# Attention output of three batches: transposed by DMA through a DRAM scratch instead of on TensorE

## The chip, the cores and the metric

One Trainium2 chip, one of its cores. The metric is the device time of one execution in microseconds (us). The kernel before took 310.94 us, the median of three runs (310.38 to 312.49).

## What is computed

Eight batches of masked attention, eight heads each, feed a two-layer network with SiLU between the layers:

```
B, H, S, D = 8, 8, 576, 64
scores = scale * q @ k.T                      # per batch and head, 576 x 576
mask_plain: 0 <= rel < 32                     # heads 0..3
mask_dil:   0 <= rel < 128 and rel % 4 == 0   # heads 4..7
attn = softmax(where(mask, scores, -1e9));  o = attn @ v
x = o.transpose(0, 2, 1, 3).reshape(4608, 512)
h = x @ w_in;  g = h * sigmoid(h);  out = g @ w_out      # 512 -> 2048 -> 512
```

Here rel is the row position minus the column position. Only a narrow band of the scores is nonzero, so the attention is cut into small blocks.

## The kernel before

**Tiles.** Everything but the accumulators is in fp16. The weights, the q and k of two batches and a ring xA stay on chip. xA holds x transposed, 128 partitions x 4 column blocks x 2048 tokens, that is the last four token groups of 512. The first layer reads it as the moving operand: `h_g_f` is one of 16 slices of the first layer of group g, four matmuls at line 895. There are ten groups: two of 256 tokens, eight of 512.

**Attention of a batch.** The score blocks (`s`, line 638) go through exp on ScalarE (lines 647 and 651) and a mask product on VectorE (line 657). The products with v are `av_p` (six plain ones of 96 rows, `P` steps) and `av_d` (two halves of four residues of 72 rows, `D` steps). All are issued at line 684. VectorE divides each by its sum (lines 687 and 688) and writes the result to `oP`, 96 x 6 x 4 x 64, or `oD`, 72 x 2 x 4 x 4 x 64. There is one oP and one oD for all batches.

**From o to x.** `oP` and `oD` hold tokens on partitions; the first layer needs features there. `x_p` (steps `XP`, line 712) transposes the 96 rows of one plain block with two TensorE transposes into PSUM. `x_d` (steps `XD`, line 728) transposes half of the dilated heads with eight. ScalarE or VectorE then copies the PSUM tile into xA (lines 516 and 518), whichever the planner thinks is free first. Per batch that makes 12 plain and 16 dilated transposes.

**q and k.** For batches 0 to 2 they are transposed on TensorE. From batch 3 on, POOL casts them to fp16 into a DRAM scratch `kq_s` (line 156), and SP issues four DMA transposes per batch from it: two into `nat` (plain heads, line 170) and two into `kqT` (dilated heads, line 173). This is a "turn". When a turn has landed, a small copy on POOL into `fence` (line 459) lets the loads of the next batch go (v, then the casts of q and k).

**Order.** The order of every engine's instructions is fixed when the kernel is built. A planner (`Plan`) keeps a modelled clock and picks the next TensorE step among attention steps, first-layer steps and second-layer steps, when its inputs and its PSUM bank are modelled as ready. DMA steps are entered with a modelled time (`yield "DMA", us`), and a first-layer step of a group depends on the steps listed in `spans` for its tokens. Each engine then executes its own list in order, and waits on semaphores for the real events. SP's list holds one load at the start and the turns of batches 3 to 7.

**Layer two.** The first two groups use plain products (line 930). The others use a scheme with seven products of halves (`y0`, `y1`, line 1005, eight matmuls per step), whose sums of operands are made on VectorE (line 966), and whose results leave through ScalarE copies (lines 1025 and 1035), VectorE additions (line 1032) and stores on ScalarE's queue (line 1037).

Of the kernel before, what the change touches and what calls it, by code (L numbers as in the profile page):

```python
# [9 lines left out]
F16 = mybir.dt.float16  # L10
# [6 lines left out]
def kernel(  # L17
# [9 lines left out]
    nc = tc.nc  # L27
    B, H, S, D = q.shape
    DM, DFF = moe_w_in.shape
    P = 128  # L30
    W = 32
    DIL = 4
    M = S // DIL
    MH = M // 2
# [3 lines left out]
    QB = P - W  # L38
    NB = S // QB
    HP = H // 2  # L40
    HN = H // 2
# [6 lines left out]
    VA, VB = 80, M - 112  # L48
    scale = 1.0 / (D ** 0.5)
    PEB = 3  # L50
    GA = 4
    NA = GA * GT
    HT = GT // 2
# [14 lines left out]
    dram = ctx.enter_context(tc.tile_pool(name="dram", bufs=1, space=bass.MemoryType.DRAM))  # L68
# [11 lines left out]
    w_out16 = cpool.tile([P, NFF, DM], F16, name="w_out16")  # L80
    xA = cpool.tile([P, HP, GA * GT], F16, name="xA")
    NP = 8
# [6 lines left out]
    oP = cpool.tile([QB, NB, HN, D], F16, name="oP")  # L89
    oD = cpool.tile([MH, 2, DIL, HN, D], F16, name="oD")  # L90
# [28 lines left out]
    mask_p = cpool.tile([P, 6, QB], F16, name="mask_p")  # L119
    mask_d = cpool.tile([P, 10, MH], F16, name="mask_d")  # L120

    kq_s = {b: dram.tile([2, H * S * D], F16, name=f"kq_s{b}") for b in range(PEB, B)}

    def nat_of(b, key):
# [4 lines left out]
    def kq_plain(b):  # L129
        t = nats[b % 2]  # L130
        return t[:, : LEAD + NW], t[:, LEAD + NW : LEAD + 2 * NW]

    def issue_nat(b, h0, h1):
        for nm, src, m0 in (("k", k, 0), ("q", q, MR)):
            rows = src[b].rearrange("h (m r) d -> m h (r d)", r=DIL)
            r0 = M - MR if nm == "k" else 0
            p0 = 0 if nm == "k" else MR
            for d, at in ((nat_of(b, nm), m0), (nat_of(b, "rest")[p0 : p0 + MR], r0)):
                nc.gpsimd.dma_start(
                    out=d[:, h0:h1].rearrange("p h r d -> p h (r d)"),  # L140
                    in_=rows[at : at + d.shape[0], h0:h1],
                )
# [18 lines left out]
    def issue_turn(b, n):  # L161
        i = n % 2
        flat = kq_s[b][i]
        if n < 2:
            if b < PEB + 2 and i == 0:
                nc.gpsimd.memset(kq_plain(b)[0][:, :LEAD], 0.0)
# [69 lines left out]
    for t in probs:  # L236
        c = 2 * 4 * MH
        n = PW + P - c
# [6 lines left out]
    for what in ORDER:  # L245
        kind, n = what[0], int(what[1])
# [4 lines left out]
        elif kind == "o":  # L251
            nc.gpsimd.dma_start(
                out=w_out16[:, 4 * n : 4 * n + 4], in_=wo[:, 4 * n : 4 * n + 4]
# [22 lines left out]
    def third_batch():  # L276
        for n in range(2, PEB):
            issue_nat(n, 0, H)
        issue_vraw(2)
        issue_vp(2)  # L280
        issue_cast(PEB)
        yield "DMA", 0.0
# [109 lines left out]
    plan = Plan()  # L392
# [15 lines left out]
    def count(key, n, then):  # L408
        counts[key] = counts.get(key, 0) + 1
        if counts[key] == n:  # L410
            then()
# [22 lines left out]
    need = {g: (t0 + n - 1) // S for g, (t0, n) in enumerate(GROUPS)}  # L434
    v_in = {b: Step(None, 0.0) for b in range(3, B)}
    turned = {b: Step(None, 0.0) for b in range(PEB, B)}

    def x_of(g):
        t0, n = GROUPS[g]
        return xA[:, :, t0 % NA : t0 % NA + n]  # L440

    def turn_gen(b):
        for n, us in enumerate((3.0, 3.0, 1.5, 7.5)):
            issue_turn(b, n)
            yield "DMA", us
        for n in (b, b + 1) if b == 3 == PEB else (b + 1,):
            if n < B:
                count(("L", n), loads_need(n), lambda n=n: start_loads(n))

    def loads_need(b):  # L450
        return 1 + (b > PEB or b == 3)
# [22 lines left out]
    def start_loads(b):  # L474
        plan.push(Step(None, 0.0), loads_gen(b), plan.now)

    def attention(b):
# [10 lines left out]
            kqT = kqTs[b % 2]  # L488
        probs_of = {}
        steps = {}  # L490
        def small(ring, shape, dt, name):
            return POOLS[ring].tile(shape, dt, tag=ring, name=name)

# [198 lines left out]
        def av_p(ring, j):  # L692
            def lhs(i):
                return prob_cols(("p", j, i // 2), i % 2)

            yield from av(
                ring, f"p{j}", oP[:, j], rcps[:, j], lhs, lambda i: vp[:, i * NB + j, : D + 1]
            )

        def av_d(ring, ab, r):  # L700
            def lhs(i):
                return prob_cols(("d", ab, r // 2, i), r % 2)

            yield from av(
                ring, f"d{ab}{r}", oD[:, ab, r], rcps[:, NB + ab * DIL + r], lhs,
                lambda i: vd[:, ab, i, r, : D + 1],
            )

        def x_p(ring, j):
            xp = small(ring, [P, HP // 2, QB], F16, f"xp_{b}_{j}")  # L710
# [29 lines left out]
        if b == 0:  # L740
            order = [
# [7 lines left out]
            ]  # L749
        elif b < ORD:  # L750
            order = [
# [6 lines left out]
            ]  # L758
        elif pe_path:
            order = [  # L760
# [7 lines left out]
            ]  # L768
        else:
            order = [  # L770
# [4 lines left out]
            ]  # L775
        for key in order:
            kind, a = key[0], key[1:]
            rings = ["x", "z"] + (["h", "y", "u"] if b == 0 else ["h"] if b < 2 else [])
# [7 lines left out]
            elif kind == "TA" and b == 0:  # L786
                st = Step(
                    lambda ring, a=a: trans_a0(ring, *a), 0.36, rings,
# [8 lines left out]
            elif kind == "TA":  # L797
                st = Step(
                    lambda ring, a=a: trans_a(ring, *a), 0.36, rings,
                    [steps["N", "k"], steps["N", "rest"]], ("ACT",),  # L800
                )
            elif kind == "TB":
                st = Step(
                    lambda ring, a=a: trans_b(ring, *a), 0.18, rings, [steps["N", "q"]], ("ACT",)
# [3 lines left out]
            elif kind == "S":  # L808
# [10 lines left out]
                else:  # L819
                    deps = [steps["TD", h] for h in range(HN)]  # L820
                st = Step(
                    lambda ring, a=a: scores(ring, *a), 0.17 + 0.32 * (b in BIASED), ["s", "hh"] + (["xz"] if pe_path else []),
# [4 lines left out]
            elif kind == "P":  # L827
                us = sorted({home["p", a[0], hp][0] for hp in range(HP // 2)})
                st = Step(
                    lambda ring, a=a: av_p(ring, *a), 0.13, rings,  # L830
# [3 lines left out]
            elif kind == "D":  # L834
                us = sorted({home["d", a[0], a[1] // 2, h][0] for h in range(HN)})
                st = Step(
                    lambda ring, a=a: av_d(ring, *a), 0.13, rings,
# [4 lines left out]
            else:  # L842
                st = Step(
                    lambda ring, a=a: x_d(ring, *a), 0.28, rings,
# [30 lines left out]
        spans = [  # L875
            (b * S + QB * key[1], b * S + QB * (key[1] + 1), steps[key])
            for key in order if key[0] == "XP"
        ] + [
            (b * S + DIL * MH * key[1], b * S + DIL * MH * (key[1] + 1), steps[key])
            for key in order if key[0] == "XD"  # L880
        ]
        return [steps[key] for key in order], spans

    gTs = {}
# [178 lines left out]
    spans = []  # L1063
# [12 lines left out]
    for c in WPARTS:  # L1076
        w_steps["sums", c] = Step(
            lambda ring, c=c: w_sums(c), 0.0, (), [max(AT_WOUT)], ("DVE",)
        )
        w_steps["last", c] = Step(  # L1080
            lambda ring, c=c: w_last(c), 0.0, (), [st for _, st in l2] + [w_steps["sums", c]], ("DVE",)
        )
    sums += [w_steps[key, c] for key in ("sums", "last") for c in WPARTS]
    n = 0
# [38 lines left out]
    while att or l1 or l2:  # L1123
# [27 lines left out]
        for q_, it, lim in cands:  # L1151
            r = plan.ready(it[1])
# [4 lines left out]
            if it[1].mate:  # L1157
# [3 lines left out]
                r = max(r, r2)  # L1161
            r = max(r, plan.t + plan.backlog(it[1].uses) - lim)
# [45 lines left out]
```

## Time and profile before

| | |
|---|---|
| median of the runs | 310.94 us |
| the profiled execution | 311.68 us |
| its span, first to last instruction | 309.9 us |
| TensorE / weight loads busy | 297.2 / 198.5 us |
| VectorE / ScalarE busy | 196.0 / 190.9 us |
| h matmuls, line 895 | 142.4 us in 640 |
| plain transposes, line 712 | 96 matmuls, 206 ns median each |
| dilated transposes, line 728 | 128 matmuls, 197 ns median each |
| copies into xA from xp / xd | 50 (32 ScalarE, 18 VectorE) / 36 (27, 9) |
| DMA transposes nat / kqT, issue to landing | 7.0 / 5.1 us median |

The page gives the busy time of each engine in one profiled execution, and a chain of waits followed back from the last instruction. The length of a matmul in the trace runs from its first read to its modelled end, and successive matmuls overlap; so what a group takes of TensorE's time is read from its start to the start of the next group. In timelines, a bracket at the end of a line gives the idle time before it and what ended it. `SPq`, `ACTq` and `POOLq` are the queues that issue DMAs.

The attention of batches 5, 6 and 7 stands at about 145 to 172, 174 to 202 and 205 to 232 us of the span; the h and y steps of groups 4 to 7 are interleaved with it.

### The profile page before, as it was taken

Reading aid. Unit: us, or ns where it says so; the run is one execution under the profiler, and the core shown is the slowest. Engines: PE = TensorE matmul, PEld = TensorE weight load, DVE = VectorE, ACT = ScalarE, POOL = GpSimd, SP = SyncE. Lnnn points to the kernel's source line nnn. Section 1 sums busy time; section 2 is a strip of 40 time slices with the busy share of each in tenths; the row PEclk is TensorE's granted clock in tenths of the full one; section 3 lists DMA queues with packets and bytes.
Section 4 is the critical chain, followed back from the end, with each engine's and each line's share of the span. In section 5 each row is a group of like instructions: output and inputs, shape, how many; then the busy total and the mean of one; then the engine's idle time right before and its main releaser. Section 6 shows DMA issues by size and latency. Waiting matters only on the chain.

```text
span 309.9 us, 7152 instructions
## 1 busy us (share of the span) xinstructions
PE 297.2 (96%) x2910; PEld 198.5 (64%) x2910; DVE 196.0 (63%) x550; ACT 190.9 (62%) x400; POOL 55.4 (18%) x83
## 2 busy tenths in 40 slices
PE   7899999989999999999999999999999999999995
PEld 3468765654567666756765775576558656756884
DVE  6278999889958784787668757666684044105411
ACT  7567783488687649668666785586572455355320
POOL 8845732001640150050005000000000000000000
PEclk9999999999999999999999999999999999999999
DMA  8999999999999999989999991101001101100131
GB/s 105 183 201 196 203 189 204 213 201 143 127 142 185 206 114 225 223 107 183 247 146 93 193 238 31 36 36 68 2 0 70 69 2 68 70 0 35 42 130 68
DMA packets 89344, 38.69 MB, mean 125 GB/s; under 512 B 61280, under 2 KB 84704, under 8 KB 89312
## 3 DMA queue, kind: packets, MB, share of 16 engines
q0 software_dynamic: 48528, 19.86, 52.6%
q1 hardware_dynamic: 35600, 8.95, 19.1%
q10 hardware_dynamic: 5184, 9.44, 8.8%
q8 instruction: 22, 0.36, 0.5%
q14 instruction: 10, 0.08, 0.1%
HBM read 39.81 MB, written 15.34 MB: 178 GB/s over the span
## 4 chain that ended last, share of the span: by engine, by line
PE 80%; DVE 10%; ACT 4%; DMA 2%; issue 1%; ACTq 1%; POOL 1%; POOLq 0%
PE h L895 35%; PE y L1005 28%; PE y L930 4%; PE s L638 3%; PE av_d L684 2%; DMA nat<-in_q_dram 2%; PE av_p L684 2%; DVE gT L909 2%; PE xp L712 2%; DVE probs L657 1%; PE s L626 1%; PE xd L728 1%; DVE work L966 1%; DVE ob L1032 1%; ACT probs L647 1%
## 5 line engine op out<-in xcount | busy, mean ns | idle before, releaser
L895 PE MATMUL h<-xA,w_in 128*128 128x512 f16 (+1 forms) x640 | 142.4, 357 | 1.8 <-ACT probs L651 0.9
L904 ACT ACTIVATE gT<-h 128x512 f16<-128x512 f32 x116 | 68.7, 597 | 43.8 <-PE h L895 42.6
L895 PEld LDWEIGHTS <-w_in 128*128 128x128 f16 x640 | 56.8, 97 | 41.2 <-issue 2.5
L1005 PEld LDWEIGHTS <-gT 128*128 128x128 f16 x512 | 49.2, 98 | 9.4 <-issue 0.4
L1032 DVE TENSOR_TENSOR ob<-y,nat 128x256 f32<-128x256 f32 x48 | 20.3, 422 | 52.2 <-PE y L1005 48.5
L1005 PE MATMUL y<-w_out,gT 128*128 128x256 f16 x384 | 48.0, 273 | 0.1
L1005 PEld LDWEIGHTS <-work 128*128 128x128 f16 x384 | 36.7, 98 | 8.9 <-issue 2.0
L1005 PE MATMUL y<-w_sum,work 128*128 128x256 f16 x256 | 31.9, 272 | 0.8 <-ACT ob L1035 0.5
L684 PEld LDWEIGHTS <-probs 128*128 128x128 f16 x448 | 23.2, 99 | 12.8 <-DVE oP L688 1.9
L647 ACT ACTIVATE probs<-s 128x768 f16<-128x768 f32 (+2 forms) x31 | 24.5, 789 | 8.3 <-PE s L638 4.4
L688 DVE TENSOR_TENSOR oD<-av_d,rcps 72x256 f16<-72x256 f32 x64 | 26.9, 421 | 2.2
L1025 ACT COPY nat<-y 128x256 f32<-128x256 f32 x48 | 17.8, 380 | 12.7 <-PE y L1005 12.5
L907 ACT ACTIVATE th<-h 128x256 f32<-128x256 f32 (+1 forms) x44 | 19.2, 445 | 7.2 <-PE h L895 4.7
L909 DVE SCALAR_TENSOR_TENSOR gT<-th,h 128x256 f16<-128x256 f32 (+1 forms) x44 | 20.6, 487 | 2.2 <-ACT th L907 2.1
L688 DVE TENSOR_TENSOR oP<-av_p,rcps 96x256 f16<-96x256 f32 x48 | 20.2, 421 | 1.6
L1035 ACT COPY ob<-y 128x256 f32<-128x256 f32 x16 | 6.0, 373 | 23.7 <-PE y L1005 22.6
L651 ACT ACTIVATE probs<-s 128x288 f16<-128x288 f32 (+2 forms) x40 | 18.0, 481 | 3.9 <-ACT ob L1035 1.9
L459 POOL COPY fence<-kqT 128x1 f16<-128x1 f16 x10 | 3.3, 334 | 87.5 <-DMA kqT<-kq_s 87.5
L687 DVE RECIPROCAL rcps<-av_d 72x4 f32<-72x4 f32 x64 | 11.1, 173 | 11.8 <-PE av_d L684 11.7
L684 PE MATMUL av_d<-vd,probs 128*128 128x65 f16 x256 | 16.8, 196 | 0.6 <-ACT probs L651 0.3
L657 DVE TENSOR_TENSOR probs<-probs,mask_p 128x768 f16<-128x768 f16 x21 | 11.6, 552 | 8.5 <-ACT probs L647 6.4
L1005 PE MATMUL y<-w_sum,gT 128*128 128x256 f16 x128 | 16.6, 273 | 0.2 <-DVE ob L1032 0.2
(100 smaller groups left out, 344.4 us busy)
## 6 DMA issues: line engine op xcount, KB each, us to landing
out_dram<-ob ACTq DMA_DIRECT2D x36, 256.0 KB, 2.3
kq_s<-in_k_dram POOLq DMA_DIRECT2D x5, 576.0 KB, 7.9
kq_s<-in_q_dram POOLq DMA_DIRECT2D x5, 576.0 KB, 10.6
vp<-in_v_dram POOLq DMA_DIRECT2D x7, 384.0 KB, 6.5
w_out<-in_moe_w_out_dram POOLq DMA_DIRECT2D x4, 512.0 KB, 10.7
vraw<-in_v_dram POOLq DMA_DIRECT2D x8, 224.0 KB, 5.0
w_in<-in_moe_w_in_dram POOLq DMA_DIRECT2D x3, 512.0 KB, 10.1
vraw<-in_v_dram POOLq DMA_DIRECT2D x8, 160.0 KB, 4.1
```

The source lines that it names most:

```text
L647: nc.scalar.activation(p2, both[:, :, :n], AF.Exp, scale=scale)
L651: nc.scalar.activation(p2[:, i], sp[i][:, :n], AF.Exp, scale=scale)
L657: nc.vector.tensor_tensor(p2, p2, mk, ALU.mult)
L684: nc.tensor.matmul(a[:, i, : D + 1], lhs(i), rhs(i), start=True, stop=True)
L688: nc.vector.tensor_tensor(o, a[:n, :, :D], rcp[:n, :, None].broadcast_to([n, HN, D]), ALU.mult)
L895: nc.tensor.matmul(h[:, :w], w_in16[:, c, f * P : (f + 1) * P], x_g[:, c], start=(c == 0), stop=(c == HP - 1),)
L904: nc.scalar.activation(gTs[g][:, f, :w], h[:, :w], AF.Silu, scale=2.0)
L907: nc.scalar.activation(th[:, :w], h[:, :w], AF.Tanh)
L909: nc.vector.scalar_tensor_tensor(gTs[g][:, f, :w], th[:, :w], 1.0, h[:, :w], ALU.add, ALU.mult)
L1005: nc.tensor.matmul(y, lhs[:, c, tb * P : (tb + 1) * P], rhs[:, c], start=first and c == 0, stop=c == KP - 1, skip_group_check=not first,)
L1025: nc.scalar.copy((t1, t5, u2)[n], y)
L1032: nc.vector.tensor_tensor(half, y, (u2, t5, t1)[n - 3], ALU.add)
```

## The change

For batches 5, 6 and 7, the steps `XP` and `XD` are left out of the order. In their place, when three plain blocks or four residues of a half have been divided, SP stores them from `oP` or `oD` to a DRAM scratch `x_s` that has the rows in token order. When both stores of a half of the batch (288 tokens) have been modelled as landed, SP issues a DMA transpose from `x_s` into xA; where the half crosses the end of the ring, two. The first layer's groups then depend on the modelled landing of these halves. Batches 0 to 4 are as before. In the diff, the store from `oP` is at the end of the step `av_p`, that from `oD` at the end of `av_d`; `parts` counts the finished pieces.

```diff
+    BYDMA = (5, 6, 7)
...
+    x_s = dram.tile([len(BYDMA) * S, DM], F16, name="x_s")
...
+    landed = {(b, ab): Step(None, 0.0) for b in BYDMA for ab in range(2)}
...
+    def x_turn(b, ab):
+        n = S // 2
+        r0 = BYDMA.index(b) * S + ab * n
+        t0 = b * S + ab * n
+        cut = min(n, NA - t0 % NA)
+        for a, z in ((0, cut), (cut, n)):
+            if a < z:
+                nc.sync.dma_start_transpose(
+                    out=xA[:, :, (t0 + a) % NA : (t0 + a) % NA + z - a], in_=x_s[r0 + a : r0 + z]
+                )
+        yield "DMA", 6.0
+
+    def x_stored(b, ab):
+        count(("O", b, ab), 2, lambda: plan.push(landed[b, ab], x_turn(b, ab), plan.now))
...
+            parts[j // 3] += 1
+            if b in BYDMA and parts[j // 3] == 3:
+                j = j // 3 * 3
+                r0 = BYDMA.index(b) * S
+                rows = x_s[r0 : r0 + S, : HN * D].rearrange("(j p) c -> p j c", p=QB)
+                nc.sync.dma_start(
+                    out=rows[:, j : j + 3],
+                    in_=oP[:, j : j + 3].rearrange("p j h d -> p j (h d)"),
+                )
+                yield "DMA", 3.0
+                x_stored(b, j // 3)
...
+            parts[2 + ab] += 1
+            if b in BYDMA and parts[2 + ab] == DIL:
+                r0 = BYDMA.index(b) * S + ab * DIL * MH
+                rows = x_s[r0 : r0 + DIL * MH, HN * D :].rearrange("(m r) c -> m r c", r=DIL)
+                nc.sync.dma_start(out=rows, in_=oD[:, ab].rearrange("p r h d -> p r (h d)"))
+                yield "DMA", 3.0
+                x_stored(b, ab)
...
+        if b in BYDMA:
+            order = [key for key in order if key[0] not in ("XP", "XD")]
...
+        if b in BYDMA:
+            n = S // 2
+            spans = [(b * S + ab * n, b * S + ab * n + n, landed[b, ab]) for ab in range(2)]
```

More of the change, by code (lines that the diff above doesn't have):

```diff
@@ L490, in attention @@
         steps = {}
+        parts = [0, 0, 0, 0]
         def small(ring, shape, dt, name):
```

## The prediction

> **What bounds the kernel.** I read the page's busy rows and slices first, then the chain of waits, then TensorE's timeline around the work that the change takes out, and last the timelines of the SP and POOL queues, because the new transfers go into SP's queue.
>
> The page, with busy time, slices and chain:
> ```profile
> span 309.9 us, 7152 instructions
> ...
> PE 297.2 (96%) x2910; PEld 198.5 (64%) x2910; DVE 196.0 (63%) x550; ACT 190.9 (62%) x400; POOL 55.4 (18%) x83
> ...
> PEclk9999999999999999999999999999999999999999
> ...
> PE 80%; DVE 10%; ACT 4%; DMA 2%; issue 1%; ACTq 1%; POOL 1%; POOLq 0%
> ```
> TensorE is busy 96% of the span at the full granted clock, and 80% of the chain that ends last is its own work. VectorE and ScalarE are near 63%: taking work from them alone is worth nothing unless TensorE is seen waiting for them.
>
> TensorE's timeline, two stretches of batches 6 and 7 (start, length, then the group):
> ```profile
> 186.03 1.89 PE L895 MATMUL h<-xA,w_in 128*128 128x512 f16 x8
> 187.75 0.25 PE L712 MATMUL xp<-ident_w,oP 96*128 96x96 f16 x2
> 187.84 0.28 PE L684 MATMUL av_d<-vd,probs 128*128 128x65 f16 x4
> ...
> 192.07 0.42 PE L728 MATMUL xd<-ident_w,oD 72*128 72x72 f16 x8
> 192.33 1.03 PE L895 MATMUL h<-xA,w_in 128*128 128x512 f16 x4
> ...
> 196.25 1.03 PE L895 MATMUL h<-xA,w_in 128*128 128x512 f16 x4
> 197.84 0.24 PE L712 MATMUL xp<-ident_w,oP 96*128 96x96 f16 x2 [0.57 <-ACT xA L516]
> ...
> 212.72 2.12 PE L1005 MATMUL y<-w_sum,work 128*128 128x256 f16 x16 [0.54 <-ACT ob L1035]
> ```
> Lengths overlap, so a group's price is the distance from its start to the next start: 187.84 - 187.75 = 0.09 us for a pair of plain transposes, 192.33 - 192.07 = 0.26 us for eight dilated ones. The row at 197.84 is a stall: four h matmuls take 0.865 us (1.72 us for the eight from 186.03 to 187.75, halved), so TensorE was free at 197.11 and waited 0.73 us, for a ScalarE copy into xA that still held the PSUM bank.
>
> SP's queue:
> ```profile
> 146.12 7.29 SPq L170 DMA_TRANSPOSE nat<-kq_s  x2
> 153.52 2.94 SPq L173 DMA_TRANSPOSE kqT<-kq_s  x2
> 175.32 5.75 SPq L170 DMA_TRANSPOSE nat<-kq_s  x2
> 181.16 4.17 SPq L173 DMA_TRANSPOSE kqT<-kq_s  x2
> ```
> POOL's queue, where the fences wait for those transposes and release the loads of the next batch:
> ```profile
> 159.93 0.19 POOL L459 COPY fence<-kqT 128x1 f16<-128x1 f16 x1 [19.86 <-DMA kqT<-kq_s]
> 162.94 0.19 POOL L459 COPY fence<-kqT 128x1 f16<-128x1 f16 x1 [2.83 <-DMA kqT<-kq_s]
> ...
> 166.77 0.79 POOL L156 DMA_DIRECT2D kq_s<-in_k_dram  x1
> ```
> The transposes of batch 6 (from 146) and 7 (from 175) are well ahead of their readers: TensorE starts the scores of these batches at 174.31 and 204.69.
>
> **What goes.** Per batch 6 pairs x 0.09 = 0.54 and 2 groups x 0.26 = 0.52, so 1.06 us, and 3.18 us for three batches. All of it lies on TensorE in a stretch (158 to 232) where it is the engine that ends last. The wait at 197.84 goes with its transpose: 0.73. Sum 3.91 us.
>
> The copies into xA go too: 19 on ScalarE and 14 on VectorE by the two programs' instruction orders, at means of 0.315/0.383 and 0.247/0.399 about 6.6 and 4.5 us of engine time. I count them at nothing, because both engines have a third of their time idle. They are worth something only where TensorE waits for these engines. Apart from 197.84 that is mainly the score stretch of batch 7, 204.59 to 214.69, where the distances between starts exceed the normal ones by 0.10, 0.44, 0.23, 0.09, 0.72 and 0.22, 1.80 us in all; the same stretch of batch 6 loses 0.34. The bound is therefore a gain of 1.8 and, as the planner reorders, a loss of as much. I take zero: in the changed order batch 6 has only two groups of y products between its first two score pairs, as batch 7 has now, and batch 7 has three, as batch 6 has now, so the cheap and the dear pattern change places.
>
> **What comes.** No TensorE, VectorE or ScalarE instruction is added. SP gets, per batch, four stores of 144 KB (96x3x512 B from oP, 72x4x512 B from oD) and two transposes of 288 KB (one of them cut in two). The nearest rows:
> ```profile
> out_dram<-ob ACTq DMA_DIRECT2D x36, 256.0 KB, 2.3
> ...
> kqT<-kq_s SPq DMA_TRANSPOSE x10, 5.1
> ```
> A store: 2.0 to 6.9 us to landing in the row of out_dram, I take 2.3. A transpose: kqT moves the same 288 KB, 4.0 to 7.9 us, I take 5.1; the issue holds SP 1.3 to 2.9. The chain from the last oD product to xA is so about 7.5 us, up to 15. Against today's starts of the readers: half (5,0) is divided at 161.6, so lands near 170 to 176, and is read at 182.06 by h of group 6; (7,0) is divided near 221 and lands at 228 to 236, read at 241.74; (7,1) is divided near 231 and read at 267.78. The next writer of oP or oD comes 20 us or more after each store. The output stores on ScalarE's queue get one more wait: SP and ACT take eight completion semaphores in turn, so each store waits for the transfer eight before it, in the changed order often one of SP's; behind it stand ScalarE's exp, silu and copies. The ones that I followed should have landed 10 us before, so I count nothing. So the added latency is hidden behind h and y work of earlier groups; with that cover gone it would cost 7.5 us per half.
>
> For the price of a transpose two rules of the Trainium skill stand against rows here. "VectorE: DVE Perf Modes" (The three transpose paths; Rules for kernel authors) speaks against the change: where PSUM will do, transpose on TensorE, 390 ns for 128x128 against 1309 ns by DMA. By it the nine squares of a half would take an estimated 11.8 us and would still land before h of group 8; the kqT row has 5.1. "Advanced Engine Details and Errata" (X-Bar Transpose) says that transposing DMAs are as fast as plain ones, which would make it 2.3; the row denies that as well.
>
> **What is moved: SP's queue.** SP works in order, and stores now stand between the transposes of q and k: the second nat transpose of batch 6 behind the store of oP rows 0 to 2 of batch 5 (ready 157.95), the second kqT behind the store of oD half 0 (ready 161.6 or, as the changed order has two more y groups there, 163). Batch 6: nat issued 158 to 162, kqT 162 to 167, landed at 170 (median) to 172. Its scores start at about 175: covered by 3 to 5 us. The POOL fence, now at 162.94, then opens at about 170, and behind it wait the v loads and the casts of batch 7, 7 us later than now. Turn 7 starts at 182 instead of 175.3; its second nat waits for oP of batch 6 (186.8), its kqT for oD (190.9), issued by 194.5, landed at 198 to 201. Readers: the plain scores near 203 and the dilated near 206. Covered by about 5 us. At nothing, then, on the path; if a landing takes 5 us more than its row, each further us is paid in full, since all that follows on TensorE is scores and work that depends on them.
>
> **Sum.** 309.9 - 3.91 = 306.0 of span. The profiled execution took 311.68, 1.78 more than its span, so 307.8 by it; the median of the runs shown is 310.94, 0.74 below that execution, so **307.1** in terms of the median.
>
> **The rivals.**
> A, the forecast: TensorE's time goes and nothing replaces it, 306.2 to 308.4 (the ends: half of the batch 7 loss saved, or 1.3 us of it doubled). For it: 96% busy and the covers above. 0.68.
> B, absorbed: the score stretches of batches 6 and 7 are set by ScalarE (a table load of 1.28 and 0.8 + 0.5 + 0.5 of exp per pair), so TensorE arrives there earlier and waits longer. With 1.8 us lost in batch 6 as well, and the 0.73 only moved, 3.91 - 1.46 - 0.73 = 1.7 is left: 309.2; at worst 310.5. Against it: before and after those stretches TensorE has y products that need no exp. 0.17.
> C, slower: SP's order. The stores hold the transposes of batch 7 back, and their chain (fence, cast, nat, kqT) has 5 us left at the scores at 203. A cast can take 16.2 instead of 8.5 us to land, the longest of the kq_s rows. It decides from 9 us of lateness on: with 12 us late, 7 are paid, 307.1 + 7 = 314; with a second such wait at batch 6 more. For it: three transfers in series that have never been in this queue; against it: DMA moves only 31 to 36 GB/s in most slices after 186 us. 0.13.
> D, that the change does not do what it says: the changed order has 84 fewer transposes and no new one, which leaves 0.02, for a gain beyond A as well.
>
> Within 1% is all that a measurement of this kernel can tell from no change; 1% is 3.1 us, so 307.8 is the border. About three quarters of A lie below it: faster 0.53. The rest of A and nearly all of B lie within: 0.32. Slower by over 1% needs C: 0.15. The range is A with B and the start of C, 306.0 to 311.5; A alone 306.2 to 308.4.
>
> **What would show it.** Right: no xp or xd rows after 158 us, h rows start to start at 0.865 through the attention of batches 5 to 7, no wait of PE h for a transfer into xA, and the first h of group 8 near 238 instead of 241.74. Wrong: PE h waiting for DMA xA<-x_s (the cover failed), PE s waiting for DMA nat or kqT (C), or longer idle before PE y and s released by ACT (B).

## The result, and the profile after

The changed kernel took 307.22 us (median of 4 runs, 306.98 to 307.81), the kernel before beside it 311.66 (4 runs, 310.38 to 312.49). The ratio is 0.9864, with a 95% interval of 0.9821 to 0.9907: 4.4 us faster. The profiled execution was one of 307.22 us with a span of 305.4. Here and below, medians and ranges are of all executions of a kernel, and the ratios leave out those that ran in a slower state, over 1.5% above the fastest.

The page of the changed kernel: span, busy rows, granted clock and the chain that ended last.
```profile
span 305.4 us, 7006 instructions
...
PE 292.1 (96%) x2826; PEld 194.0 (64%) x2826; DVE 192.7 (63%) x536; ACT 185.6 (61%) x381; POOL 55.5 (18%) x83
...
PEclk9999999999999999999999999999999999999999
...
PE 78%; DVE 10%; DMA 5%; ACT 3%; issue 2%; ACTq 1%; POOL 1%; DVEq 0%; POOLq 0%
```
TensorE has lost exactly 84 instructions and 5.1 us of busy time, of which 3.28 lie in the stretch that was changed (below), and is still busy 96% at the full clock. One share of the chain has grown: DMA went from 2% to 5%.

TensorE's timeline of the changed kernel, at the places that answer to those shown of before:
```profile
190.58 0.29 PE L703 MATMUL av_p<-vp,probs 128*128 128x65 f16 x4
190.70 1.89 PE L937 MATMUL h<-xA,w_in 128*128 128x512 f16 x8
192.43 0.28 PE L703 MATMUL av_p<-vp,probs 128*128 128x65 f16 x4
192.55 1.89 PE L937 MATMUL h<-xA,w_in 128*128 128x512 f16 x8
...
236.59 1.89 PE L937 MATMUL h<-xA,w_in 128*128 128x512 f16 x8
```
No xp or xd row is left here, eight h matmuls take 1.73 us from start to start, and the stall at 197.84 is gone. The first h of group 8 starts at 236.59. Before, it started at 241.58 by the same view (the prediction's 241.74 is 0.16 us late, and so is its 267.78 for group 9, which starts at 267.62).

For the account I cut both traces at the same two events, the first av_p of batch 5 and the first h of group 8. One line of the windows view of each kernel (stretch; its length; then busy us and instructions of PE, PEld, DVE, ACT and POOL; granted clock; DMA share; GB/s). The kernel before:
```profile
155.89:241.58 85.69, 83.74 (x835) 55.74 (x832) 57.10 (x165) 55.12 (x109) 4.69 (x7) 1.00 0.49 81
```
The changed kernel:
```profile
155.16:236.59 81.43, 80.46 (x751) 52.77 (x748) 53.36 (x151) 49.97 (x90) 5.26 (x7) 1.00 0.69 135
```
The stretch is 4.26 us shorter: 3.28 of TensorE's busy time and 0.98 of its idle time (1.95 to 0.97). The same cut in a second profile of the changed kernel (the experiment e12 below) gives 80.91, so 4.78 shorter. Outside the stretch nothing was changed: the changed kernel reached its start 0.73 us earlier and took 0.49 us longer behind its end. That is chance: in the other profiles whose order is the same up to there, the starts lie between 154.66 and 156.4, and the last parts between 68.08 and 68.81 us.

One wait that went with it is not among the rows of the prediction. TensorE's timeline of the kernel before, among the y products behind the attention of batch 7:
```profile
232.12 1.92 PE L1005 MATMUL y<-w_out,gT 128*128 128x256 f16 x16
234.22 1.03 PE L1005 MATMUL y<-w_sum,gT 128*128 128x256 f16 x8 [0.19 <-DVE ob L1032]
...
235.97 1.04 PE L1005 MATMUL y<-w_sum,work 128*128 128x256 f16 x8
237.22 1.03 PE L1005 MATMUL y<-w_sum,work 128*128 128x256 f16 x8 [0.21 <-ACT nat L1025]
```
Sixteen of these products take 1.75 us from start to start and eight take 0.87, so 0.35 and 0.38 us are lost here. In the changed kernel they run without a gap.

The two lines of the windows view also show the price: DMA is now busy 69% of this stretch instead of 49%. The DMA issues of the changed kernel (count, KB each where a size is given, median us from issue to landing):
```profile
out_dram<-ob ACTq DMA_DIRECT2D x36, 256.0 KB, 3.2
...
x_s<-oP SPq DMA_DIRECT2D x6, 144.0 KB, 2.3
...
kqT<-kq_s SPq DMA_TRANSPOSE x10, 3.6
...
xA<-x_s SPq DMA_TRANSPOSE x7, 3.2
```
In the median the new transfers are quick. Medians of this row do not compare like with like, though: in the trace of the changed kernel the view finds a landing for only 19 of the 36 output stores and 3 of the 7 transposes into xA. The 3.2 for an output store against 2.3 before is no measure of the change; between 150 and 240 us the view gives 2.7 in both kernels. What counts is single transfers. One of the transposes that the view leaves out, issued at 180.44, has its last completion update in the trace 6.0 us later.

SP's queue in the changed kernel:
```profile
157.25 0.33 SPq L723 DMA_DIRECT2D x_s<-oP  x1
157.68 2.41 SPq L172 DMA_TRANSPOSE nat<-kq_s  x1
160.20 1.26 SPq L175 DMA_TRANSPOSE kqT<-kq_s  x1
162.49 1.00 SPq L742 DMA_DIRECT2D x_s<-oD  x1
163.59 1.48 SPq L175 DMA_TRANSPOSE kqT<-kq_s  x1
...
182.46 3.95 SPq L172 DMA_TRANSPOSE nat<-kq_s  x1
191.97 2.89 SPq L175 DMA_TRANSPOSE kqT<-kq_s  x2
```
POOL's queue in the changed kernel:
```profile
167.09 0.84 POOL L477 COPY fence<-kqT 128x1 f16<-128x1 f16 x1 [3.19 <-DMA kqT<-kq_s]
...
170.62 0.79 POOL L158 DMA_DIRECT2D kq_s<-in_k_dram  x1
171.40 0.77 POOL L158 DMA_DIRECT2D kq_s<-in_q_dram  x1
```
The stores do stand between the transposes of q and k, the fence opens 4 us later than before (162.94), and the casts of batch 7 are issued at 170.62 instead of 166.77. TensorE waits for none of it: the trace has no wait of PE for nat, kqT or xA in this stretch.

Somebody else pays. The chain of the changed kernel holds one long transfer, and VectorE's timeline shows who waits for it. From the chain:
```profile
177.38 8.04 DMA out_dram<-ob
```
From ScalarE's queue and VectorE's timeline:
```profile
176.55 0.34 ACTq L1079 DMA_DIRECT2D out_dram<-ob  x1
177.38 0.34 ACTq L1079 DMA_DIRECT2D out_dram<-ob  x1
...
182.82 0.42 DVE L1074 TENSOR_TENSOR ob<-y,nat 128x256 f32<-128x256 f32 x1 [1.03 <-PE y L1047]
...
185.52 0.76 DVE L1074 TENSOR_TENSOR ob<-y,nat 128x256 f32<-128x256 f32 x2 [0.83 <-DMA out_dram<-ob]
```
From TensorE's timeline:
```profile
181.76 1.03 PE L1047 MATMUL y<-w_out,gT 128*128 128x256 f16 x8
183.29 1.03 PE L1047 MATMUL y<-w_out,gT 128*128 128x256 f16 x8 [0.49 <-DVE ob L1074]
```
There are two ob tiles, and ScalarE stored them at 176.55 and 177.38. The casts of batch 7, issued at 170.62 and 171.40, need 10.3 and 14.0 us to land (to 185.4), so both stores run beside them and take 6.1 and 8.0 us. VectorE cannot write the next ob before. At 185.52 the page says so. At 182.82 it names PE, but the product that this step adds had ended a microsecond before; the first store's landing, 176.55 + 6.1 = 182.65, fits. TensorE then waits for the y bank that VectorE has not emptied: 181.76 to 183.29 is 1.53 us where 0.87 is normal.

The same place in the kernel before, from ScalarE's queue and VectorE's timeline:
```profile
178.05 0.34 ACTq L1037 DMA_DIRECT2D out_dram<-ob  x1
...
179.96 0.34 ACTq L1037 DMA_DIRECT2D out_dram<-ob  x1
...
184.06 0.42 DVE L1032 TENSOR_TENSOR ob<-y,nat 128x256 f32<-128x256 f32 x1 [0.75 <-PE y L1005]
...
185.98 0.42 DVE L1032 TENSOR_TENSOR ob<-y,nat 128x256 f32<-128x256 f32 x1 [0.41 <-PE y L1005]
```
There the casts had landed by 177.9, before the first store began. The stores took 3.0 and 5.4 us, and each tile was written again 6.0 us after its store was issued, so the second had 0.6 us to spare. The late landing is therefore not wholly new. Other output stores of the kernel before took up to 6.9 us while q and k were being moved, and nobody waited for them.

### The profile page after: what moved, and what is told of

It is laid out like the page before. It is cut to its first block, busy times and chain, and to the rows that moved or that the text cites. A ratio compares the mean times of both kernels' runs of the same rounds, so it can differ in the third digit from the quotient of the medians.

```text
span 305.4 us, 7006 instructions
## 1 busy us (share of the span) xinstructions
PE 292.1 (96%) x2826; PEld 194.0 (64%) x2826; DVE 192.7 (63%) x536; ACT 185.6 (61%) x381; POOL 55.5 (18%) x83
## 4 chain that ended last, share of the span: by engine, by line
PE 78%; DVE 10%; DMA 5%; ACT 3%; issue 2%; ACTq 1%; POOL 1%; DVEq 0%; POOLq 0%
PE h L937 36%; PE y L1047 27%; PE y L972 4%; PE s L657 3%; DMA out_dram<-ob 3%; PE av_d L703 2%; DMA nat<-in_q_dram 2%; DVE gT L951 2%; PE av_p L703 1%; DVE probs L676 1%; DVE ob L1074 1%; DVE oD L707 1%; DVE oP L707 1%; PE xp L749 1%; ACT th L949 1%
## 5 line engine op out<-in xcount | busy, mean ns | idle before, releaser
L937 PE MATMUL h<-xA,w_in 128*128 128x512 f16 (+1 forms) x640 | 140.6, 357 | 1.8 <-ACT probs L670 0.9
L937 PEld LDWEIGHTS <-w_in 128*128 128x128 f16 x640 | 57.7, 97 | 44.4 <-issue 2.7
L1047 PEld LDWEIGHTS <-gT 128*128 128x128 f16 x512 | 49.0, 98 | 10.3 <-issue 1.1
L1047 PE MATMUL y<-w_out,work 128*128 128x256 f16 x128 | 16.6, 273 | 0.0
## 6 DMA issues: line engine op xcount, KB each, us to landing
w_out<-in_moe_w_out_dram POOLq DMA_DIRECT2D x4, 512.0 KB, 10.3
```

The costliest lines, as they stand in the source:

```text
L937: nc.tensor.matmul(h[:, :w], w_in16[:, c, f * P : (f + 1) * P], x_g[:, c], start=(c == 0), stop=(c == HP - 1),)
L1047: nc.tensor.matmul(y, lhs[:, c, tb * P : (tb + 1) * P], rhs[:, c], start=first and c == 0, stop=c == KP - 1, skip_group_check=not first,)
```

## The experiments

Two theories go in. Mine: the gain is TensorE's transposes and the waits around them, and all of the DMA work is hidden. The rivals: the gain is that of the copies, or of queue positions; or the change costs something that the gain covers up. All edits are made to the changed kernel unless said. The kernel before was run beside each: 312.16, 312.48 and 312.28 us in the groups e1 to e4, e5 to e8 and e9 to e12.

**e1: the transposes alone come back.**
```diff
-            order = [key for key in order if key[0] not in ("XP", "XD")]
 # in x_p and x_d, after the transposes and before the copies
+            if b in BYDMA:
+                return
```


> The changed kernel with the 84 TensorE transposes of batches 5 to 7 put back where they stood, but without their copies into xA (nothing reads what they write; x still comes by DMA). Theory (the gain is TensorE's own time, 3.2 us of it transposes and about 1 us of waits): 310 to 311 us, 0.994 to 1.000 of before, that is at least 2.5 us more than the changed kernel's 307.2. Rival (the gain comes from the 33 copies that ScalarE and VectorE no longer make): it stays at 307 to 308, 0.986 to 0.989 of before.

Measured: 310.39 us (309.16 to 311.92), ratio 0.995 (0.9921 to 0.9979). Against the changed kernel's 0.9864 that is 0.9% lost, about 2.7 us, where the transposes' own time is 3.18. TensorE's time is most of the gain. e1 is not free of late stores either: in its trace VectorE waits 2.1 us for one.

**e2: the copies alone come back**, 14 on ScalarE and 19 on VectorE (the kernel before had 19 and 14), from constant masks into a spare tile that nobody reads.
```diff
+                for c0, c1, t in x_pieces(QB * j, QB):
+                    eng = yield best(0.17, 0.22)
+                    copy_on(eng, spare[:, :2, : c1 - c0], mask_p[:, 2:4, : c1 - c0])
+                return
...
+                    for hp in range(HP // 2):
+                        eng = yield best(0.365, 0.36)
+                        copy_on(
```


> The changed kernel with 33 copies of the old widths put back on ScalarE and VectorE at the places of the old copies, from a constant tile to a spare one (nothing reads them), but without TensorE transposes. Theory: 307 to 308.3 us, 0.986 to 0.991 of before; at most the waits of TensorE that went with the copies (about 1 us) come back. Rival (copies): 310 to 311.5, back at before.

Measured: 307.71 us (307.24 to 307.85), 0.9874 (0.9842 to 0.9906). No cost that can be seen, so the copies were rightly counted at nothing. Yet e1 beats the kernel before, which has the copies and not the DMA work, by 0.5%. So transposes and copies together seem to cost more than the two apart; e1 also has another order, so this is not isolated. One place of it is the row at 197.84, a transpose that waits for a copy to leave its PSUM bank, and it needs both.

**e3: each DMA transpose into xA issued twice.**
```diff
-            if a < z:
+            for _ in range(2 if a < z else 0):
```


> The changed kernel with each transpose from x_s into xA issued twice, one after the other, the same data to the same place. Each half then lands about 3 us later and SP is held 1.3 to 1.9 us longer per half. Theory (the DMA path is hidden with 8 us or more to spare): 306.8 to 308, the same as the changed kernel. Rival (the path is at the edge): each of the six halves shows up to 3 us on TensorE, 310 or more.

Measured: 307.41 us (306.53 to 308.78), 0.9873 (0.9834 to 0.9911). For the half that is cut in two, SP is held 8.44 us where it took 3.5, and the last transposes of q and k of batch 7 are issued up to 201 instead of 195; the time does not move. The path from oD to xA has cover to spare, as the prediction said.

**e4: the stores to the scratch issued by POOL.**
```diff
-                nc.sync.dma_start(
+                nc.gpsimd.dma_start(
...
-                nc.sync.dma_start(out=rows, in_=oD[:, ab].rearrange("p r h d -> p r (h d)"))
+                nc.gpsimd.dma_start(out=rows, in_=oD[:, ab].rearrange("p r h d -> p r (h d)"))
```


> The changed kernel with the stores into x_s issued from POOL's queue and not from SP's. SP's transposes of q and k of batches 6 and 7 then no longer stand behind stores, so the fence of batch 6 should open about 4 us earlier (163 and not 167) and the v loads and casts of batch 7 should have left the window of 177 to 186 us, where the changed kernel shows an output store that took 8 us to land and TensorE losing about 2 us in the scores of batch 6. Theory that SP's order causes that loss: 306 to 307, 0.982 to 0.986 of before, and no wait of VectorE for DMA out_dram there. Rival (the loss belongs to the score stretch, whatever the DMAs do): 307.2, the same as the changed kernel.

Measured: 307.81 us (306.47 to 311.52), 0.9878 (0.9829 to 0.9927). As a test of SP's order it failed, because it moved the delay and did not remove it. From POOL's timeline of e4:
```profile
168.95 0.33 POOL L477 COPY fence<-kqT 128x1 f16<-128x1 f16 x2
```
The fences now stand behind a store at 168.26 that waits for VectorE, and the casts leave at 172.08, later than in the changed kernel. What SP's order alone costs was not isolated.

**e5, e6, e7: one, four and five batches by DMA.**
```diff
-    BYDMA = (5, 6, 7)
+    BYDMA = (7,)               # e5
+    BYDMA = (4, 5, 6, 7)       # e6
+    BYDMA = (3, 4, 5, 6, 7)    # e7
```


> Only batch 7 by DMA (two of its transposes of 288 tokens, one cut in two, after all turns and casts are over). Theory: a third of the transposes, 1.06 us, and the share of TensorE's waits that hang on the score stretch of batch 7: 309.3 to 311 against a before of about 312 on this chip, 0.990 to 0.997. If the gain comes all from one place and not per batch, it is either 1.000 or 0.987.

> Batch 4 by DMA as well, whose attention runs while the DMA engines are 90% busy or more (the slices from 95 to 178 us). Theory (transposes cost TensorE about 1.1 us per batch and the landing stays hidden): 0.982 to 0.985 of before, 1 us faster than the changed kernel. Rival (with the DMA engines busy, x lands late, or the turns and loads behind it do): 0.987 or more, with TensorE seen waiting for a DMA into xA, nat or kqT.

> Batches 3 and 4 by DMA as well. Theory: 0.979 to 0.983 of before, 2 us faster than the changed kernel. Rival (busy DMA engines): 0.987 or more, with TensorE waiting for xA, nat or kqT.

Measured: e5 310.75 us, 0.9949 (0.9928 to 0.9971), about a third of the gain, as expected. In its trace too a store, issued at 180.29 beside transposes of q and k, takes 6.7 us; VectorE waits 1.1 us for it, although the casts are issued at 167.54 and 168.32, near their old place. e6 308.39, 0.9893 (0.9842 to 0.9943): no further gain. e7 317.11, 1.0124 (1.0074 to 1.0174): slower than before. Both of the last two miss my theory, by which every further batch was worth about another 1 us. The waits of e6 and e7 show no wait of PE for a transfer into xA or for the transposed q and k, so it is not the rival of late transposes either. What they show, in TensorE's and VectorE's timeline of e7 and ScalarE's queue:
```profile
150.66 0.34 ACTq L1079 DMA_DIRECT2D out_dram<-ob  x1
...
159.20 0.42 DVE L1074 TENSOR_TENSOR ob<-y,nat 128x256 f32<-128x256 f32 x1 [3.80 <-DMA out_dram<-ob]
...
159.68 1.65 PE L1047 MATMUL y<-w_sum,gT 128*128 128x256 f16 x7 [3.40 <-DVE ob L1074]
```
A store issued at 150.66 holds its tile until 159.2; VectorE waits 3.8 us for it and TensorE 3.4 for VectorE. In all, PE waits 6.6 us for ob in e7 (4 times). The stretch behind it in the windows view of e7 (columns as above) shows a second cost:
```profile
155.00:170.00 15.00, 11.60 (x87) 7.06 (x85) 5.98 (x20) 5.09 (x9) 0.00 (x0) 0.77 1.25 214
```
TensorE is idle 3.4 of 15 us, and the granted clock of this stretch is 0.77 where the changed kernel had 1.00. Why it falls here was not tested.

So a new theory: the output stores are slowed by the DMA work that the change shifts and adds, and two output tiles are too few to cover that. In the changed kernel itself I expected little from it.

**e8: a third output tile.**
```diff
-            ob = o32.tile([P, DM], F32, tag="ob", name=f"ob_{g}_{tb}")
+            ob = o32.tile([P, DM], F32, tag="ob", name=f"ob_{g}_{tb}", bufs=3)
 # and the same at the other place where ob is taken
```


> The changed kernel with three output tiles ob in place of two, so that a store that takes 8 us to land, as the one at 177 us did, holds nobody. Theory (the 2 us that TensorE loses in the scores of batch 6 come from the order of exp, y products and table load, not from the store): at most 0.3 us gained, 0.986 to 0.989 of before. Rival (the late store causes the loss): 0.980 to 0.984.

Measured: 305.52 us (304.69 to 306.48), 0.9784 (0.975 to 0.9817). This is the fastest version of the study, and it lies with the rival, which put the price at the late stores, and somewhat beyond it. The order of instructions on every engine is that of the changed kernel, so only the tile differs. In e8 the two stores are issued at 176.81 and 177.64 and land as slowly (5.8 us for the first; for the second the view has no landing, but its last completion update comes 7.9 us after its issue). Nobody waits for them. VectorE's timeline of e8:
```profile
182.01 0.42 DVE L1074 TENSOR_TENSOR ob<-y,nat 128x256 f32<-128x256 f32 x1
...
183.80 0.74 DVE L1074 TENSOR_TENSOR ob<-y,nat 128x256 f32<-128x256 f32 x2
```
This also answers a rival: that the changed order asks for the tiles sooner. VectorE is ready for the next ob 5.2 and 6.2 us after the two stores are issued; in the kernel before both were 6.0. With landings of 3.0 and 5.4 us, as before, neither would have been waited for. TensorE's timeline of e8 at the place of the stall at 183.29:
```profile
182.02 1.91 PE L1047 MATMUL y<-w_out,gT 128*128 128x256 f16 x16
183.77 0.28 PE L703 MATMUL av_p<-vp,probs 128*128 128x65 f16 x4
```
The sixteen products run without a gap. The whole stretch of e8, in the windows view:
```profile
155.42:235.58 80.16, 79.86 (x750) 52.81 (x748) 53.24 (x151) 50.13 (x90) 5.26 (x7) 1.00 0.73 138
```
0.30 us of idle TensorE is left of 80.16, with DMA as busy as before the edit (0.73 and 0.69).

**e9 to e12: does the third tile help by itself, and does it carry the longer lists?** e9 is the kernel before with `bufs=3`, e10 and e11 are e7 and e6 with it, and e12 is the changed kernel again.

> The kernel before (all transposes on TensorE), with three output tiles ob in place of two. This tells whether the third tile repairs a cost of the change or is a gain of its own. Theory 1 (late stores are a cost that the change brings, since it pushes the casts of the next batch into the time of the stores): 0.998 to 1.002, no gain here. Theory 2 (stores are late in both): 0.990 to 0.994, the same 0.8% as in the changed kernel.

> Batches 3 to 7 by DMA with three output tiles. In the run with two, VectorE waited 8.1 us for output stores that landed late, up to 3.8 us each, and TensorE behind it. Theory (late stores are what made that run slow): 0.975 to 0.985, at least 8 us less than the 317 us. Rival (SP's order or the late loads do it, the stores are a symptom): 1.000 to 1.012, with TensorE then waiting for nat, kqT, xA or v.

> Batches 4 to 7 by DMA with three output tiles. Theory (late stores): 0.973 to 0.977, 1 us less than three batches with three tiles. Rival: 0.980 to 0.990.

> The changed kernel once more, beside these on the same chip: 0.985 to 0.989 of before, for the comparison with the runs of three tiles.

| | kernel | us | ratio to before, 95% |
|---|---|---|---|
| e9 | before, three tiles | 311.49 | 0.9993 (0.997 to 1.0016) |
| e12 | batches 5 to 7, two tiles | 308.46 | 0.9879 (0.9843 to 0.9915) |
| e8 | batches 5 to 7, three tiles | 305.52 | 0.9784 (0.975 to 0.9817) |
| e11 | batches 4 to 7, three tiles | 306.51 | 0.9832 (0.9798 to 0.9866) |
| e10 | batches 3 to 7, three tiles | 309.96 | 0.9899 (0.9853 to 0.9945) |

e9 is the control that counts: without the change a third tile shows no gain, at most 0.3% by its interval. So e8 adds little or no gain of its own; it repairs a cost that the change brings. In e12 VectorE's timeline names the store at both places:
```profile
181.92 0.42 DVE L1074 TENSOR_TENSOR ob<-y,nat 128x256 f32<-128x256 f32 x1 [0.63 <-DMA out_dram<-ob]
...
184.50 0.76 DVE L1074 TENSOR_TENSOR ob<-y,nat 128x256 f32<-128x256 f32 x2 [0.70 <-DMA out_dram<-ob]
```
e10 recovers 7 of the 12 us between e7 and e8 and stays behind e8; its profiled execution, at 313.62 us well above its median, is no more than a hint that output stores are still waited for (4.7 us in one place). It is also the only trace in which TensorE waits for a transpose into xA, 0.9 us. e11 missed: VectorE waits for no output store any more, but four batches are about 1 us slower than three by the medians, with intervals that overlap. Its trace loses about 2 us in the score stretch of batch 5 (142 to 153), where PE waits for ob of VectorE (0.83 us) and of ScalarE (0.56), so, with no store in the way, for the order of their work. Why the planned order is worse there was not settled.

That the casts are what slows the two stores is read from the overlap, and no run isolates it: e4 was to do so and failed. The times fit closely. The second store lands at 185.42 and the second cast at 185.4; in e12 VectorE goes on at 184.50 and that cast, issued at 170.91, takes 13.5 us. In the kernel before, the second store, at 179.96 + 5.4, lands just ahead of a transpose of q and k, at 178.22 + 7.4. e5 shows that such a wait can come without moved casts.

## Why the prediction was right, and which of its steps were not

It gave 307.1 us, and 307.22 was measured. The closeness is partly chance: 307.1 was counted from a median of 310.94 for the kernel before, which became 311.66 with the fourth run. The saving is the fairer measure: 3.91 us were forecast, and 4.4 were measured by the medians, 4.5 by the spans and 4.26 in the changed stretch. Point by point:

- **TensorE's transposes, 3.18 us.** Right: 3.28 of busy time left the stretch, and putting them back (e1) costs about 2.7.
- **The wait at 197.84, 0.73.** Right, but incomplete: the 0.73 us lost between batch 7's y products at 232 to 237 (rows released by ob and nat) vanished as well. The sum had no term for it.
- **Copies at nothing.** Right for the copies by themselves (e2).
- **The score stretches change places, net zero.** Right in its sum, and by luck. The losses were 0.34 and 1.80 us in batches 6 and 7, and are about 2.0 and 0.45 after. But of the 2.0 some 1.25 hang on the late stores, 0.66 of them the stall for ob at 183.29. In e8, without these, the losses are 0.76 and 0.45: batch 7 did become cheap, batch 6 did not become dear, and 0.9 us were to be gained where the sum has nothing.
- **The chain from oD to xA.** Hidden, as said, with enough cover for double the transposes (e3). Its price was too high: 5.1 was taken, 3.2 is the median of those the view gives, and 6.0 the slowest. The Trainium skill's "Advanced Engine Details and Errata" (X-Bar Transpose) has transposing DMAs as fast as plain ones. From 200 to 240 us of the changed kernel two whole transposes into xA landed in 3.2 and 3.7 us and output stores of 256 KB in 2.2 in the median: nearer than the 5.1 against 2.3 that I held up, but not equal. The kqT row is 3.6 in the changed kernel, over half of its transfers, and 5.1 again in e4; what makes it dear was not tested. The estimate of 11.8 from "VectorE: DVE Perf Modes" is denied by 3.2 and by 6.0 alike.
- **SP's queue.** Right in what it cost: turn 7 from 182.46 (182), its last transposes issued by 194.9 (194.5), and no wait of TensorE. The 182 is right in part by chance: the fence opened at 167.09 and not at 170, so the casts left 4 us later and not 7, but the first of them took 10.3 us to land and not 8.5, and SP was then busy with a transpose into xA from 180.44 for 1.91 us. Two readings were off without weight: "DMA moves only 31 to 36 GB/s in most slices after 186 us" holds for 4 of 16 slices of that row, which go from 0 to 130, and only one of the six halves, not one per batch, is cut in two. Rival C, the slower case, looked at the wrong victim: even in e7, which is slower, no transpose of q or k is waited for.
- **The step that failed: "The POOL fence, now at 162.94, then opens at about 170, and behind it wait the v loads and the casts of batch 7, 7 us later than now."** I saw the shift (it came to 4 us) and asked only whether the casts would still reach TensorE in time. I did not ask whom they meet on the way. They meet the output stores, and with two ob tiles stores that take 6.1 and 8.0 us instead of 3.0 and 5.4 stop VectorE and then TensorE. For the stores I had asked only what ScalarE's queue waits for, and wrote "I count nothing".

The size of that cost is 0.8 to 0.95% by the ratios of e8 against the changed kernel's two measurements, 2.5 to 3 us of the kernel before. That is rough, as the intervals of e8 and of the changed kernel nearly touch (0.9817 and 0.9821). The traces place only part of it. From the last score group of batch 6 (the row of 20 s<-kqT matmuls) to the av_p group that answers to the row at 190.58, the changed kernel takes 11.68 us, e12 11.16, e3 11.04, e4 11.19 and e8 10.41, so 0.6 to 1.3 us lie there; the spans of the profiled executions differ by 0.5 to 1.7. Where the rest of the difference between the medians goes is open.

So the number was right for two reasons and one compensation. The transposes and one wait are worth what was worked out, 3.18 and 0.73. A further wait of 0.73 went that was not counted, and so did 0.9 of the score stretches; the late stores, not counted either, took 1.25 back. That makes 4.3, where the stretch became 4.26 shorter. Without the last term it makes 5.5, and in e8 the stretch is 5.53 shorter. By the ratios the change without the late stores is worth 2.2% (e8), more than the forecast's range allowed.

## What to carry to other kernels

When a change moves DMA work, list who shares the DMA engines in the new place, and find among them the transfer with the fewest buffers behind it: here it was the output stores, which no row of before shows anybody waiting for. Price TensorE's groups from start to start, and do not take a gain per batch for granted: three batches gained, a fourth gave nothing more and a fifth lost it all, and a third tile made neither of them better than three batches. A repair needs its control on the old kernel; only e9 turns "the third tile is faster" into "the change makes the third tile worth having".

## What the runs showed that was not expected

A 256 KB store, which takes 2.0 us in the median from 195 us on in the kernel before, took 8.0 us beside two casts. DMA transposes stretch as well: one of 288 KB took 3.2 us in a quiet part of the changed kernel and another 6.0 beside the casts, and a 256 KB piece of one took 13.5 in e7, with the DMA engines nearly full. A median over landings hides this where the view finds few of them, and those mostly from quiet stretches. The releaser that a timeline names can be the wrong one: the steps that write ob at 182.82 in the changed kernel and at 184.06 in e4 (idle 1.05 us, put down to PE) both start within 0.2 us of the landing of the store that held the tile, 182.65 and 177.77 + 6.2 = 183.97.
